# GEGLU block: the first 512 rows of x by transposing transfers, unit 0 for both halves ahead of unit 1's raw products

## Chip, cores and metric

One core of one Trainium2 chip. The time is that of one launch on the device in microseconds, the median of three runs. All five engines (TensorE = PE, VectorE = DVE, ScalarE = ACT, GpSimd = POOL, SyncE = SP) have an instruction queue of their own and wait for each other by semaphores.

## What is computed

```python
B, S, Dm, Df = 1, 2048, 1024, 3584      # all bf16
def reference(x, w_gate, w_up, w_down):
    g = jnp.einsum("bsd,df->bsf", x, w_gate)
    u = jnp.einsum("bsd,df->bsf", x, w_up)
    h = _gelu(g) * u                     # tanh form
    return jnp.einsum("bsf,fd->bsd", h, w_down)
```

## The kernel before

The 2048 rows of x are two passes p of two halves c of N = 512 rows. Dm is NKB = 8 blocks of 128 rows of the weights; PE needs x with these blocks on the partitions, so x is transposed: `XT[p, c][k]` is block k, 128 partitions by 512 rows. Df is 28 blocks of 128, taken in pairs: a *unit* u is 256 columns of w_gate and of w_up (`load_w(u)`).

Most of the work goes by Strassen-like products (seven for eight), whose operands are sums of blocks. For a unit, `s1` to `s4` are sums and differences of its weights' quarters, `sa` a cast of one; `t1` to `t4` are those of x's halves, `tb` a cast. They are made by DVE, POOL and ACT in fp32r, and PE multiplies them: `product(e, s2, t2)` and so on in `unit`. *Raw products* (`raw_products`) are products of bf16 weights and bf16 x as they came, needed by each unit before its sums; their first part is copied to `p1` by ACT (`snap`).

Unit 0 for pass 0 is made without sums (`plain`), since nothing can be made before x and weights are there: per half 32 products of 128x512, into banks 0 to 3 for half 0 and banks 4 to 7 for half 1. `finish` takes gelu of the gate banks (ACT), multiplies by the up banks (DVE) and stores to DRAM (SP).

The order is written out by hand: the queues of SP, DVE, POOL and PE keep the program's order, and ACT's too inside the blocks shown. All DMAs are issued by SP's queue, in program order, and each of eight semaphores in turn goes with a DMA: a DMA is issued only when the one eight before it has landed.

The start, as before.py has it:

- PE warms itself with 7 products of constants (`keep_warm`, line 871).
- SP issues four copies of 128 rows of x (line 797), then unit 0's weights in six pieces (line 817, row blocks 0-2, 2-5, 5-8 of gate and up), unit 1's weights (line 148), four *transposing* transfers for rows 512 to 1023 of x (line 811, 256 columns each, that is two row blocks of `XT[0, 1]`), unit 2's weights (line 146), and then those for rows 1024 on (`turn_some`).
- PE transposes the first 512 rows, 8 blocks for each of the four copies (`turn`, line 804), against an identity that POOL makes, into banks 4 to 7; DVE and ACT copy the result to `xT0` (line 807).
- PE: `plain` for half 0, first two row blocks in column halves of 256; unit 1's raw products; `plain` for half 1 (`rest_of_0`, called from the first item's `aside`); then unit 1's f32 products `s2 t2`, `s1 t1`, `s3 t3`, `s4 tb`.
- DVE makes unit 1's sums s1, s2, s4, then t1, t2, t3, t4. POOL makes s3, and then waits for t4 (`pool_behind`, line 198) before it begins the sums of unit 2.

The kernel's later part (the joint units of both passes, and the product with w_down) is not touched.

Of the kernel before, what the change touches and what calls it, by code (L numbers as in the profile page):

```python
# [7 lines left out]


@with_exitstack  # L10
def kernel(
# [31 lines left out]
    NS = N // P  # L43
    NPASS = S // (2 * N)
    NU = NFB // 2
    NWARM = 7
    JOINT = 3
    AHEAD = {(0, -2): 2, (0, -1): 2, (0, 1): 1, (1, -2): 1}
    DIVIDED7 = 5
# [21 lines left out]

    xT = [xpool.tile([P, NKB, N], bf16, name=f"xT{p}") for p in range(NPASS)]
    XT = {(p, 0): [xT[p][:, k] for k in range(NKB)] for p in range(NPASS)}
    XT2 = {(p, 0): lambda k, p=p: xT[p][:, k : k + 2] for p in range(NPASS)}
    h = [[None, None], [None, None]]

    wdn = w_down.rearrange("(kh j p) d -> p kh j d", kh=2, p=P)
# [10 lines left out]
    def late_half(p):  # L88
        if p:
            tile = hpool.tile([P, NJ, N], bf16, name="h01")  # L90
            XT[p, 1] = [tile[:, k] for k in range(NKB)]
            x_late.append(tile[:, :NKB])
            XT2[p, 1] = lambda k: tile[:, k : k + 2]
        else:
            tiles = [slot([P, 2, N], bf16, "x") for _ in range(KH)]
            XT[p, 1] = [tiles[k // 2][:, k % 2] for k in range(NKB)]
            XT2[p, 1] = lambda k: tiles[k // 2]

    def new_h(kh, c):
        h[kh][c] = hpool.tile([P, NJ, N], bf16, name=f"h{kh}{c}")  # L100
# [685 lines left out]


    warm = nc.const_aps.tensor(1.0, [P, N], bf16)
    ident = xpool.tile([P, P], bf16, name="ident")
    make_identity(nc, ident)  # L790

    def load_x(c):
        t = []
        for i in range(NS):
            xn = slot([P, Dm], bf16, "xn")
            r0 = c * N + i * P
            nc.sync.dma_start(out=xn, in_=x2[r0 : r0 + P, :])  # L797
            t.append(xn)
        return t

    def turn(xn, i):
        tp = bank[4 + i].bitcast(bf16).rearrange("p (k r) -> p k r", k=NKB)
        for ko in range(NKB):
            nc.tensor.transpose(tp[:, ko, :], xn[i][:, ko * P : (ko + 1) * P], ident)  # L804
        for ks in (range(NKB),) if i < NS - 1 else (range(KH), range(KH, NKB)):
            ks = slice(ks.start, ks.stop)
            (on_act if i == 1 else on_dve)(out=xT[0][:, ks, i * P : (i + 1) * P], in_=tp[:, ks])

    def transposing(p, c, k0):
        r0 = (2 * p + c) * N  # L810
        nc.sync.dma_start_transpose(
            out=XT2[p, c](k0), in_=x2[r0 : r0 + N, k0 * P : (k0 + 2) * P]
        )

    def load_wf(queue, k0, k1):
# [7 lines left out]
            if queue is not nc.sync:  # L823
                tc.keep_in_program_order(got)

    xn0 = load_x(0)
    wf = wpool.tile([P, 2, NKB, 2 * P], bf16, name="w")
    for k0, k1 in ((0, 2), (2, 5), (5, NKB)):
        load_wf(nc.sync, k0, k1)
    w = load_w(1)  # L830
    late_half(0)
    for ko in range(0, NKB, 2):
        transposing(0, 1, ko)
    ahead = load_w(2, True)
    late_half(1)
    turns = [(c, ko) for ko in range(0, KH, 2) for c in (1, 0)] + [(c, ko) for c in (1, 0) for ko in range(KH, NKB, 2)]
# [5 lines left out]

    turn_some(2)

    def plain(ps, c, kos, parts=1):
        n = N // parts
        for k in range(kos.start, kos.stop, 2):
            for part in range(parts):
                cols = slice(part * n, (part + 1) * n)
                for p, (j, i) in zip(ps, [(j, i) for j in range(2) for i in range(2)]):  # L850
                    for ko in (k, k + 1):
                        matmul(
                            p[:, cols],
                            wf[:, i, ko, j * P : (j + 1) * P],
                            XT[0, c][ko][:, cols],
                            ko == 0 and part == 0,
                            ko == NKB - 1,
                        )

# [1 line left out]
        for j in range(2):  # L861
            times(0, j, c, gelu(ps[2 * j]), ps[2 * j + 1])

    on_dve, on_act = nc.vector.tensor_copy, nc.scalar.copy
    s = sums_s(w, dve)
    t = sums_t(0, dve, lambda name: slot([P, N], f32r, name))
    T = [t, None]
    with tc.manual_schedule(engines={ENG.Activation}):
        def keep_warm(n, cols):
            for _ in range(n):  # L870
                nc.tensor.matmul(
                    bank[3][:, :cols], lhsT=warm[:, :P], rhs=warm[:, :cols], start=True, stop=True
                )

        keep_warm(NWARM, N)
        for i in range(NS):
            if i == 2:
                keep_warm(2, 2 * P)
            turn(xn0, i)
        plain(bank[0:4], 0, range(0, 2), parts=2)  # L880
        plain(bank[0:4], 0, range(2, NKB))
        s["s3"] = sums_s(w, pool)["how"]["s3"](s)
        s["s1"] = s["how"]["s1"](s, range(1))
        finish(bank[0:4], 0)
        s["s1"] += s["how"]["s1"](s, range(1, 2))
        nxt = {"p1": raw_products(odd, cc, 0, w)}
        s.make("sa", "s2", "s4")
        t.make("t1")

    seen = xpool.tile([P, 1], f32, name="seen")  # L890

    def rest_of_0(part):
        if part == 0:
            plain(bank[4:8], 1, range(NKB))
            t.make("t2", "tb")
        else:
            t3 = t["how"]["t3"](t, range(0, 2))
            finish(bank[4:8], 1)
            t["t3"] = t3 + t["how"]["t3"](t, range(2, KH))

    spots, twos = {}, {}

# [165 lines left out]
    with tc.manual_schedule(engines={ENG.Activation}):  # L1068
        for n, (u, p) in enumerate(items):
            first = n == 0  # L1070
            def after_p5():
                at_p5(n)

            def aside(part):
                if first and part < 0:
                    rest_of_0(part + 2)
                if first and part == 0:
                    t.make("t4")
                for v in loads.get((n, part), ()):
                    ws[v] = load_w(v, True)  # L1080
                turn_some(AHEAD.get((n, part), 0))
                if (n, part) == (1, -2):
                    two_sums("t2", XL[:, KH:], "t1")
                    two_sums("t3", XL[:, KH:], XL[:, :KH])

            def mid():
                if "sa" not in ss[u]:
                    ss[u]["sa"] = sums_s(loaded(u), pool)["how"]["sa"](None)

            def ahead_of_p4():  # L1090
                if n == 0:
                    raw_of(2, 0, even, cc)()
                elif n == 1:
                    p1 = [raw_first(e, 1, loaded(v)) for e, v in ((Eb, 2), (D, 1))]
                    raw_second(K, 1, loaded(2))
                    finish_raw(2, 1, K, p1[0])

                    T[1]["tb"] = spots["tb"]
                    for k in range(KH):
                        nc.scalar.copy(out=spots["tb"][k], in_=XT[1, 1][KH + k])  # L1100
                    new_room(0, 1, *["t4"] * KH, *["n"] * 3)
                    two_sums("t4", xT[1][:, KH:], "t2")
                    new_s(0, "s1", "s2", "s3", "s4")

                    def second_half():
                        raw_second(K, 1, loaded(1))
                        finish_raw(1, 1, K, p1[1])

                    nxt["c11"] = second_half
                elif n == 3:  # L1110
                    raw_of(0, 1, Ea, D)()

            def behind_p4():
                if "c11" in nxt:
                    nxt.pop("c11")()

            def p4(c12):
                times(p, 2 * u, 1, gelu(c12[0]), c12[1])
                if n == len(items) - 1:
                    split_b_rest("tb")  # L1120
                    more_room()
                    split_b("t4")
                whole_p4(u, p, banks[0], ss[u], ahead_of_p4, behind_p4)
                if n == len(items) - 1:
                    split_b_rest("t4")

            if first:
                banks = odd, cc, dd
                late = lambda: add(cc, nxt["p1"])
            else:  # L1130
                banks = (Eb, D, K) if n == 3 else (Ea, K, D)
                late = None
            unit(u, p, banks, ss[u], late, after_p5, aside, mid, p4)
            ss[u].pop("sa")
            if n == 1:
                Ea, Eb, K, D = Eb, D, K, Ea
            elif n == 3:
                Ea, Eb, K, D = Ea, K, D, Eb

# [68 lines left out]
```

## Time and profile before

| | |
|---|---|
| median of 3 runs | 526.49 us (526.41 to 526.50) |
| profiled execution, its own time | 526.39 us |
| its span, first to last instruction | 524.6 us |
| granted PE clock, mean | 1.00 |
| PE busy | 518.7 us (99%) |
| DVE, ACT, POOL busy | 390.6, 293.6, 336.9 us |
| HBM read, written | 72.61 MB, 29.62 MB |

In rows of the timeline the first number is the start in us from the span's start, the second the time from the start of the first to the end of the last of the merged instructions; then engine (SPq is SP's queue, issuing), line, operation, output<-inputs and shapes, how many, and in brackets how long the engine had been idle and what ended that. In rows of the chain: start, length, what. In windows: the stretch, its length, busy time and number of instructions of each engine, granted PE clock, share of the 16 DMA engines, GB/s. Matmuls' ends are modelled, and a few matmul records are missing.

### The profile page before, as it was taken

The page shows a single profiled execution, that of the slowest core. Times are in us where ns is not written, and L with a number is a line of the kernel's source. Part 1 is how long each engine was busy: PE and PEld are TensorE (multiplying, and loading weights), DVE is VectorE, ACT ScalarE, POOL GpSimd, SP SyncE. Part 2 cuts the span into 40 slices and gives each one's busy share as a digit, 9 for nine tenths or more (in the row PEclk, how much of TensorE's full clock was granted, in tenths as well). Part 3 has the DMA queues.
Part 4 walks back from the last instruction along what each step waited for, and adds up shares of the span by engine and source line. Part 5 has one row for each costly group of instructions (what it writes and reads, how often), then busy time and mean ns, then how long its engine had stood idle before and what let it go on. Part 6 is the DMA issues. An engine that isn't in the chain of part 4 may idle for free.

```text
span 524.6 us, 7866 instructions
## 1 busy us (share of the span) xinstructions
PE 518.7 (99%) x2356; PEld 368.0 (70%) x2389; DVE 390.6 (74%) x598; ACT 293.6 (56%) x542; POOL 336.9 (64%) x339
## 2 busy tenths in 40 slices
PE   9999999999999999999999999999999999999997
PEld 5576877767667676767677676754788885488887
DVE  2984553687888989897988889897789226967934
ACT  3556655676778687878787787851135602142430
POOL 1079999998999999999999999840000000000594
PEclk9999999999999999999999999999999999999999
DMA  9961323032625457373727444999976999993732
GB/s 252 213 166 52 89 84 111 32 109 92 191 81 181 123 180 230 112 239 111 233 92 231 163 159 159 343 374 415 385 259 212 394 398 353 392 327 101 238 133 71
DMA packets 102730, 105.91 MB, mean 202 GB/s; under 512 B 19360, under 2 KB 80800, under 8 KB 102688
## 3 DMA queue, kind: packets, MB, share of 16 engines
q1 hardware_dynamic: 102688, 105.41, 61.4%
q8 instruction: 19, 0.31, 0.3%
q14 instruction: 23, 0.19, 0.1%
HBM read 72.61 MB, written 29.62 MB: 195 GB/s over the span
## 4 chain that ended last, share of the span: by engine, by line
PE 98%; DMA 1%; issue 0%; SPq 0%; DVE 0%
PE bank L127 98%; DMA xn<-in_x_dram 1%; SPq L797 0%; PE bank L804 0%; DVE st L106 0%
## 5 line engine op out<-in xcount | busy, mean ns | idle before, releaser
L127 PE MATMUL bank<-h,s 128*128 128x512 f32 x500 | 132.6, 395 | 0.0
L109 POOL TENSOR_TENSOR q<-q 128x256 fp32r<-128x256 f32 x28 | 26.6, 984 | 144.4 <-DMA q<-td 143.8
L127 PEld LDWEIGHTS bank<-h,s 128*128 128x128 f32 x500 | 93.9, 188 | 21.1
L127 PE MATMUL bank<-xT,w 128*128 128x512 bf16 (+1 forms) x446 | 106.8, 376 | 1.5
L127 PEld LDWEIGHTS <-w 128*128 128x128 bf16 x504 | 45.4, 98 | 59.1 <-issue 11.9
L109 POOL TENSOR_TENSOR s<-w 128x512 fp32r<-128x512 bf16 (+1 forms) x76 | 77.8, 1040 | 10.4 <-DMA w<-in_w_gate_dram 10.3
L127 PE MATMUL bank<-t,s 128*128 128x512 f32 x276 | 76.5, 400 | 0.0
L127 PE MATMUL bank<-q 128*128 128x512 f32 x264 | 65.6, 390 | 0.0
L127 PEld LDWEIGHTS bank<-t,s 128*128 128x128 f32 x276 | 51.9, 188 | 12.1
L127 PEld LDWEIGHTS bank<-q 128*128 128x128 f32 x264 | 49.6, 188 | 10.4
L123 ACT COPY p<-bank 128x512 f32<-128x512 f32 x72 | 40.6, 589 | 28.9 <-PE bank L127 28.6
L106 DVE TENSOR_TENSOR q<-h,h 128x512 fp32r<-128x512 bf16 x56 | 38.3, 684 | 16.8 <-DMA h<-hd 16.8
L123 ACT COPY u<-bank 128x512 f32<-128x512 f32 x62 | 35.8, 589 | 21.1 <-PE bank L127 21.0
L109 POOL TENSOR_TENSOR s<-s,s 128x256 fp32r<-128x256 f32 x60 | 44.8, 769 | 1.6
L106 DVE TENSOR_TENSOR xz<-bank,xz 128x512 f32<-128x512 f32 x44 | 30.2, 691 | 18.2 <-PE bank L127 14.6
L127 PEld LDWEIGHTS <-h 128*128 128x128 bf16 x224 | 21.7, 98 | 26.5 <-issue 0.5
L109 POOL TENSOR_TENSOR s<-w,s 128x512 fp32r<-128x512 bf16 (+1 forms) x37 | 39.4, 1081 | 0.0
L109 POOL TENSOR_TENSOR s<-s,w 128x512 fp32r<-128x512 f32 (+1 forms) x37 | 37.3, 1024 | 0.9
L118 ACT CAST tb<-raw 128x512 fp32r<-128x512 bf16 x28 | 16.9, 632 | 36.0 <-DMA raw<-in_w_down_dram 26.5
L109 POOL TENSOR_TENSOR m<-raw,m 128x512 fp32r<-128x512 bf16 x28 | 34.5, 1234 | 2.2
L106 DVE TENSOR_TENSOR bank<-bank,u 128x512 f32<-128x512 f32 x49 | 33.7, 688 | 0.0
L106 DVE TENSOR_TENSOR v<-bank,v 128x512 f32<-128x512 f32 x44 | 29.2, 684 | 2.1 <-PE bank L127 1.7
(122 smaller groups left out, 911.7 us busy)
## 6 DMA issues: line engine op xcount, KB each, us to landing
raw<-in_w_down_dram SPq DMA_DIRECT2D x68, 256.0 KB, 4.0
q<-td SPq DMA_DIRECT2D x66, 256.0 KB, 5.4
td<-m SPq DMA_DIRECT2D x42, 256.0 KB, 2.8
hd<-o SPq DMA_DIRECT2D x80, 128.0 KB, 1.7
h<-hd SPq DMA_DIRECT2D x17, 512.0 KB, 6.9
hd<-h SPq DMA_DIRECT2D x30, 128.0 KB, 1.7
h<-hd SPq DMA_DIRECT2D x5, 768.0 KB, 9.0
out_dram<-st SPq DMA_DIRECT2D x30, 128.0 KB, 4.6
```

Source lines behind the costliest of these rows:

```text
L106: nc.vector.tensor_tensor(out=out, in0=a, in1=b, op=op)
L109: nc.gpsimd.tensor_tensor(out=out, in0=a, in1=b, op=op)
L118: nc.scalar.copy(out=t, in_=src)
L123: nc.scalar.copy(out=t, in_=ps)
L127: nc.tensor.matmul(ps, lhsT=lhs, rhs=rhs, start=start, stop=stop, skip_group_check=True)
```

## The change

The first 512 rows of x also come by transposing transfers of 256 columns, four, and they are first in SP's queue. Unit 0's weights come in eight pieces (two row blocks of gate, of up, four times) from ACT's queue, ahead of ACT's other work. In SP's queue unit 1's weights stand behind all eight transposing transfers. The copies of x, the identity, PE's transposes and their evictions are gone; PE warms with 8 products. `plain` takes the row blocks in pairs, the gate's two banks first and then the up's, always 512 columns wide, for half 0 and then at once for half 1; unit 1's raw products follow. DVE makes t1 first, then t2, half of t3, s1, s2, the rest of t3, and s4 and t4 behind unit 1's raw sum; ACT makes `tb` and `sa` ahead of the second half's gelu; POOL makes s3 when unit 1's weights are there.

```diff
-    NWARM = 7
+    NWARM = 8
+    FIRST = (0, 2), (2, 4), (4, 6), (6, NKB)
...
-    xn0 = load_x(0)
     wf = wpool.tile([P, 2, NKB, 2 * P], bf16, name="w")
-    for k0, k1 in ((0, 2), (2, 5), (5, NKB)):
-        load_wf(nc.sync, k0, k1)
-    w = load_w(1)
+    for k0, k1 in FIRST:
+        load_wf(nc.scalar, k0, k1)
+    for k0, k1 in FIRST:
+        transposing(0, 0, k0, k1 - k0)
     late_half(0)
     for ko in range(0, NKB, 2):
         transposing(0, 1, ko)
+    w = load_w(1)
     ahead = load_w(2, True)
...
-    def plain(ps, c, kos, parts=1):
-        n = N // parts
-        for k in range(kos.start, kos.stop, 2):
-            for part in range(parts):
-                cols = slice(part * n, (part + 1) * n)
-                for p, (j, i) in zip(ps, [(j, i) for j in range(2) for i in range(2)]):
+    def plain(ps, c):
+        for k in range(0, NKB, 2):
+            for i in range(2):
+                for j in range(2):
                     for ko in (k, k + 1):
                         matmul(
-                            p[:, cols],
+                            ps[2 * j + i],
                             wf[:, i, ko, j * P : (j + 1) * P],
-                            XT[0, c][ko][:, cols],
-                            ko == 0 and part == 0,
+                            XT[0, c][ko],
+                            ko == 0,
                             ko == NKB - 1,
                         )
...
         keep_warm(NWARM, N)
-        for i in range(NS):
-            if i == 2:
-                keep_warm(2, 2 * P)
-            turn(xn0, i)
-        plain(bank[0:4], 0, range(0, 2), parts=2)
-        plain(bank[0:4], 0, range(2, NKB))
+        plain(bank[0:4], 0)
+        plain(bank[4:8], 1)
+        t.make("t1")
+        finish(bank[0:4], 0)
+        t.make("t2", "tb")
+        t3 = t["how"]["t3"](t, range(0, 2))
         s["s3"] = sums_s(w, pool)["how"]["s3"](s)
-        s["s1"] = s["how"]["s1"](s, range(1))
-        finish(bank[0:4], 0)
-        s["s1"] += s["how"]["s1"](s, range(1, 2))
+        s.make("s1", "sa", "s2")
+        finish(bank[4:8], 1)
+        t["t3"] = t3 + t["how"]["t3"](t, range(2, KH))
         nxt = {"p1": raw_products(odd, cc, 0, w)}
-        s.make("sa", "s2", "s4")
-        t.make("t1")
...
-    def rest_of_0(part):
-        if part == 0:
-            plain(bank[4:8], 1, range(NKB))
-            t.make("t2", "tb")
-        else:
-            t3 = t["how"]["t3"](t, range(0, 2))
-            finish(bank[4:8], 1)
-            t["t3"] = t3 + t["how"]["t3"](t, range(2, KH))
...
             def aside(part):
-                if first and part < 0:
-                    rest_of_0(part + 2)
                 if first and part == 0:
+                    s.make("s4")
                     t.make("t4")
```

More of the change, by code (lines that the diff above doesn't have):

```diff
@@ L6 @@
 from concourse._compat import with_exitstack
-from concourse.masks import make_identity
 @with_exitstack
@@ L73 @@
     XT = {(p, 0): [xT[p][:, k] for k in range(NKB)] for p in range(NPASS)}
-    XT2 = {(p, 0): lambda k, p=p: xT[p][:, k : k + 2] for p in range(NPASS)}
+    XT2 = {(p, 0): lambda k, n, p=p: xT[p][:, k : k + n] for p in range(NPASS)}
     h = [[None, None], [None, None]]
@@ L92, in late_half @@
             x_late.append(tile[:, :NKB])
-            XT2[p, 1] = lambda k: tile[:, k : k + 2]
+            XT2[p, 1] = lambda k, n: tile[:, k : k + n]
         else:
@@ L96, in late_half @@
             XT[p, 1] = [tiles[k // 2][:, k % 2] for k in range(NKB)]
-            XT2[p, 1] = lambda k: tiles[k // 2]
+            XT2[p, 1] = lambda k, n: tiles[k // 2]
     def new_h(kh, c):
@@ L788, with transposing @@
     warm = nc.const_aps.tensor(1.0, [P, N], bf16)
[L789 to L793, printed above, removed]
-        for i in range(NS):
[L795 to L809, printed above, removed]
+    def transposing(p, c, k0, nk=2):
         r0 = (2 * p + c) * N
         nc.sync.dma_start_transpose(
-            out=XT2[p, c](k0), in_=x2[r0 : r0 + N, k0 * P : (k0 + 2) * P]
+            out=XT2[p, c](k0, nk), in_=x2[r0 : r0 + N, k0 * P : (k0 + nk) * P]
         )
@@ L862, in finish @@
             times(0, j, c, gelu(ps[2 * j]), ps[2 * j + 1])
-    on_dve, on_act = nc.vector.tensor_copy, nc.scalar.copy
     s = sums_s(w, dve)
@@ L875 @@
         keep_warm(NWARM, N)
-        for i in range(NS):
-            if i == 2:
-                keep_warm(2, 2 * P)
-            turn(xn0, i)
-        plain(bank[0:4], 0, range(0, 2), parts=2)
-        plain(bank[0:4], 0, range(2, NKB))
+        plain(bank[0:4], 0)
[4 more added lines that the diff above has]
+        t3 = t["how"]["t3"](t, range(0, 2))
         s["s3"] = sums_s(w, pool)["how"]["s3"](s)
-        s["s1"] = s["how"]["s1"](s, range(1))
-        finish(bank[0:4], 0)
-        s["s1"] += s["how"]["s1"](s, range(1, 2))
+        s.make("s1", "sa", "s2")
+        finish(bank[4:8], 1)
+        t["t3"] = t3 + t["how"]["t3"](t, range(2, KH))
         nxt = {"p1": raw_products(odd, cc, 0, w)}
-        s.make("sa", "s2", "s4")
-        t.make("t1")
     seen = xpool.tile([P, 1], f32, name="seen")
-    def rest_of_0(part):
-        if part == 0:
-            plain(bank[4:8], 1, range(NKB))
-            t.make("t2", "tb")
-        else:
-            t3 = t["how"]["t3"](t, range(0, 2))
-            finish(bank[4:8], 1)
-            t["t3"] = t3 + t["how"]["t3"](t, range(2, KH))
     spots, twos = {}, {}
```

## The prediction, made before the changed kernel ran

> **What bounds the kernel now.** I read the page's head and chain first, then the chain's start, then the timeline of the first 30 us.
>
> ```profile
> span 524.6 us, 7866 instructions
> PE 518.7 (99%) x2356; PEld 368.0 (70%) x2389; DVE 390.6 (74%) x598; ACT 293.6 (56%) x542; POOL 336.9 (64%) x339
> ...
> PE 98%; DMA 1%; issue 0%; SPq 0%; DVE 0%
> ```
> ```profile
> 2.12 4.03 DMA xn<-in_x_dram
> ...
> 6.20 0.62 PE bank L804 x8
> ...
> 7.08 1.70 PE bank L127 x14
> ...
> 8.84 10.74 PE bank L127 x49
> ```
> The chain is PE from 6.2 us to the end. Only its first 6.2 us are anything else: the four copies of x. So the change can move the end only by the moment from which PE runs without a gap, or by a gap that it opens; every edit lies in the first 30 us.
>
> ```profile
> 0.74 1.82 SPq L797 DMA_DIRECT2D xn<-in_x_dram  x4
> 0.77 3.15 PE L871 MATMUL bank<-const-bfloat16-1.0 128*128 128x512 bf16 x7 [0.77 <-PEq L1192]
> 3.71 1.30 PE L804 MATMUL bank<-ident,xn 128*128 128x128 bf16 x16
> 4.85 0.38 PE L871 MATMUL bank<-const-bfloat16-1.0 128*128 128x256 bf16 x2
> 5.50 1.32 PE L804 MATMUL bank<-ident,xn 128*128 128x128 bf16 x16 [0.27 <-DMA xn<-in_x_dram]
> 6.66 10.76 PE L127 MATMUL bank<-xT,w 128*128 128x256 bf16 x55
> 7.97 7.67 SPq L811 DMA_TRANSPOSE x<-in_x_dram  x4
> 17.25 7.07 PE L127 MATMUL bank<-x,w 128*128 128x512 bf16 x31
> 23.97 5.82 PE L127 MATMUL bank<-t,s 128*128 128x512 f32 x24
> ```
> Before 17.25 us PE has unit 0's first half (32 products of 512 columns, the first eight as sixteen of 256) and 16 raw products. From 8.84 to 19.58 there are 49 records and one gap in them, 50 steps: 0.216 us each. Counting 16 of these back from 17.25 gives 13.8 us as the end of unit 0's first half. From there 16 + 32 products lead to 24.2 us, where the first f32 product can begin (the row's 23.97 is within one product of it). This 13.8 is the mark: in both kernels 48 dense products follow before the f32 ones, only in another order. The end moves by what the mark moves, if nothing behind it becomes late.
>
> **The change, part by part.** Removed: four copies of x, the identity, 32 PE transposes (1.30 + 1.32 us) with two short warming products, and their evictions by DVE and ACT. They lie in PE's first 6.7 us, which end on x's arrival, so removing them gives nothing until something better arrives. Added: one warming product, (3.71 - 0.77)/7 = 0.42 us, so warming ends at 4.1 us; hidden if the first x comes later.
>
> x's first half now comes by four transposing transfers, first in SP's queue; unit 0's weights by eight 128 KB transfers, first in ACT's queue. Products of pair k of row blocks wait for transfer k and both of its weight pieces. Eight products of a pair take 8 x 0.216 = 1.73 us.
>
> ```profile
> L811 SPq DMA_TRANSPOSE xT<-in_x_dram x1: 1237/1237/1237, 38.1 to 38.1; - x1
> ...
> DMA to landing us min/median/max: 3.1/3.1/3.1
> ```
> This one, alone, landed 3.1 us after issue. The first x could land at 0.74 + 3.1 = 3.9 us; beside weights, twice its 1.24 us share, 5.1. PE would start some 1.5 us earlier than 6.66. But then it needs a pair each 1.73 us. What a pair costs is read from windows of transfers:
>
> ```profile
> core 0: us, PE busy (x) PEld busy (x) DVE busy (x) ACT busy (x) POOL busy (x), PEclk, DMA share, GB/s
> 0.00:2.00 2.00, 1.23 (x3) 0.44 (x4) 0.00 (x0) 1.27 (x1) 0.70 (x6) 1.00 0.04 7
> 10.00:12.00 2.00, 2.00 (x11) 0.90 (x10) 0.49 (x1) 0.00 (x0) 0.44 (x1) 1.00 1.21 290
> 12.00:13.00 1.00, 1.00 (x7) 0.45 (x5) 0.20 (x1) 0.29 (x1) 1.00 (x1) 1.00 1.35 211
> 13.00:14.00 1.00, 1.00 (x6) 0.43 (x5) 0.66 (x1) 0.73 (x2) 0.84 (x2) 1.00 1.25 280
> 16.00:18.00 2.00, 2.00 (x11) 0.94 (x10) 2.00 (x5) 1.35 (x3) 0.00 (x0) 1.00 1.17 50
> 18.00:19.00 1.00, 1.00 (x7) 0.41 (x6) 1.00 (x2) 0.55 (x2) 0.00 (x0) 1.00 0.84 198
> 22.00:23.00 1.00, 1.00 (x6) 0.49 (x5) 1.00 (x3) 0.00 (x0) 0.00 (x0) 1.00 1.47 219
> 26.00:27.00 1.00, 1.00 (x6) 0.84 (x5) 1.00 (x3) 0.80 (x2) 0.00 (x0) 1.00 1.07 234
> 40.80:41.20 0.40, 0.40 (x3) 0.33 (x2) 0.00 (x0) 0.40 (x2) 0.40 (x1) 1.00 0.00 0
> ```
> The last columns are the share and GB/s. Weight copies alone move 290; transposing transfers alone 234 to 280; where the two meet (12:13, 18:19, 22:23) 211, 198, 219, mean 209; and 16:18, in the middle of transposing ones, fell to 50. No row shows both kinds from two queues at once. Bounds: 280 to 290 if they don't disturb each other, 100 or less if they stall each other; I take 209, the nearest rows. The first half needs 1.05 MB of x and 1.05 MB of weights: 2.10/0.209 = 10.0 us from 2.0 us (the first window moved 7 GB/s) = 12.0. Last packet to landing I take as 0.6: the transfer issued at 38.1 landed at 41.2, and 40.8:41.2 moved nothing. So the last pair lands at 12.6, its products end at 14.4: **+0.6 us** on the mark.
>
> Beside this row stands the Trainium skill, "DMA: Bandwidth & Descriptors", section "Latency and other measured facts": a transposing transfer's effective rate is 261 GB/s. By it, and 290 for copies, the last pair would land at about 10.2 and the mark would be 2 us earlier; the windows 22:23 and 12:13 don't agree, since there copies stand beside it.
>
> Pairs then come each 0.52 MB/0.209 = 2.5 us against 1.73 of work: PE waits 0.8 us between them. In the trace PE's products take 0.42 us each until 4 us and 0.216 afterwards, while the column PEclk reads 1.00 in both: a half rate which that column does not show. PE gets to 4.1 us warm, idles until about 5.1, and then works some two thirds of the time. If one pair falls back to the half rate it takes 3.4 us, 1.0 more than the transfers need; that cost is nothing if it never happens, 1.7 in the last pair, 3 for two pairs. I take **+1.0 us**.
>
> Behind the mark, with its cover:
> - x's second half: four more transposing transfers from 12.6 on, 0.262/0.234 = 1.1 us each against 1.73 of products. Hidden; without it each late one costs its lateness.
> - Unit 1's weights now come behind all eight: 12.0 + 4 x 1.1 + 1.05/0.29 = 20.0, landed at 20.6. Raw products need the first at 14.4 + 6.9 = 21.3. Slack 0.7 us.
> - ACT's order puts the casts of these weights ahead of the gelus of the second half and the copies p of the raw products, for which the first f32 product waits.
>
> ```profile
> 13.57 0.60 ACT L221 ACTIVATE g<-bank 128x512 f32<-128x512 f32 x1 [0.27 <-PE bank L127]
> ...
> 15.41 1.29 DVE L106 TENSOR_TENSOR s<-s,w 128x512 fp32r<-128x512 f32 x2
> ...
> 16.21 1.14 ACT L118 CAST sa<-w 128x512 fp32r<-128x512 bf16 x2
> ...
> 27.43 2.49 DVE L106 TENSOR_TENSOR t<-xT,t 128x512 fp32r<-128x512 bf16 x4
> ...
> 29.98 0.18 POOL L198 COPY seen<-t 128x1 f32<-128x1 f32 x1 [15.46 <-DVE t L106]
> ...
> 31.67 3.40 PE L127 MATMUL bank<-xT,w 128*128 128x512 bf16 x15
> ...
> 39.11 4.30 POOL L109 TENSOR_TENSOR h<-h,xT 128x1024 fp32r<-128x1024 bf16 x2
> ```
> Casts 20.6 to 21.7, then four of 0.6 us: 24.1, needed at 14.4 + 6.9 + 3.5 = 24.8. Covered by 0.7 us.
> - DVE: s1, s2 move behind t2, s4 behind the raw sum. Of s1 and s2 four of 1.29/2 us follow the landing at 20.6: 23.2, before 24.8. t4 releases POOL, before at 29.98, 5.8 us after 24.2. Now two raw sums, two of s4 and four of t4 (2.49) follow the raw products' end: 4 x 0.65 + 2.5 = 5.1 us behind the f32 start. No cost.
> - Transfer waits of the new order: the last weight piece is issued only when the second x has landed (about 7.5), 3 us before use; the fourth x waits for the first. Hidden.
> - SP: the transposing transfers for rows 1024 on are queued behind stores that wait for both finished halves, about 24 us; POOL reads them at 39.1 us. Hidden by 10 us. Unit 2's weights follow unit 1's by 3.6 us, 24.2; PE reads them at 31.7. Hidden.
>
> Sum: +0.6 +1.0 = +1.6 on a profiled execution of 526.39 us (span 524.6 and 1.8 around it); the median of the runs, 526.49, is 0.1 above. Rounded: **527.9**, own range 527.0 to 528.8.
>
> **Rivals.** A difference within 0.2% (1.05 us) is about what a measurement of this kernel can't tell from none.
> 1. *Two queues fill the engines, no loss.* For: 280 and 290 GB/s alone; against: the meeting rows. From 245 to 285 GB/s the last pair lands at 11.2 to 10.0, the mark falls at 12.9 to 11.9 (no earlier, as 5.1 + 6.9 = 12.0): -0.9 to -1.9, **525.1**. It decides when the last pair lands before 12.1 us. Faster.
> 2. *PE keeps its full rate through the waits.* Only +0.6 (or -0.9 to +0.6 with a better rate): **526.9**. The rule of the Trainium skill, "TensorE: Matmul & The Clock Gate", section "Part 1: The HAM clock gate", says this: the rate falls after an idle window of about 3.4 us, and gaps of 0.8 are shorter. For it in the trace: PE idled from 5.1 to 5.5 and the products behind ran at 0.216.
> 3. *Weights of unit 1 late.* A stall as in 16:18 (2 us at 50 instead of 209: 1.5 us lost) in either stream uses up the 0.7 us of slack, and the casts hold up gelus and copies on ACT: +1.6 + 1.5 = **529.5**.
> 4. *It doesn't do what it says*: the queue's slot waits make ACT's weights follow x in turn. Then the streams are not beside each other, and the sum is rival 1's lower rate, about 526.
>
> **How the numbers follow.** Forecast 0.40 (slower), rival 3 0.15 (slower), rival 1 0.25 (faster), rivals 2 and 4 0.20 (within). So faster 0.25, within 0.20, slower 0.55. The range takes in most of rivals 1 and 3: 525.0 to 529.9.
>
> **What would show it.** In the profile after: first bf16 product on xT near 5 us; then pairs of eight with waits on the transposing transfers; windows of 5 to 12 us near 209 GB/s with both kinds of transfer; the last of the first 32 products near 14 to 15 us; products 0.42 us apart somewhere after 5 us; the first f32 product near 25.8 against 24.2; no other gap to the end. Wrong if the first 32 products end before 13 us, if 0.42 never recurs, or if PE shows a wait on s, t or w behind the raw products.

## The result, and the profile after

The changed kernel takes 527.41 us (median of 18 runs, 526.94 to 528.15), the kernel before, run beside it, 526.55 (18 runs, 526.21 to 527.48): a ratio of 1.0018, 95% interval 1.001 to 1.0025. It is 0.5 to 1.3 us slower: the way that was forecast, by about half of the 1.6 us. The profiled execution took 527.61 us against 526.39.

The head and the chain's shares on the page of the changed kernel, and the waits of PE that the trace lists (total, times, longest, in us):

```profile
span 525.8 us, 7806 instructions
PE 520.0 (99%) x2348; PEld 365.6 (70%) x2348; DVE 388.8 (74%) x594; ACT 290.7 (55%) x540; POOL 338.0 (64%) x337
...
PE 93%; DVE 0%; issue 0%
```
```profile
PE bank L127 <- DMA xT<-in_x_dram: 1.7, 2, 1.4
...
PE bank L127 <- DVE h L106: 0.4, 1, 0.4
```

PE's share of the chain fell from 98 to 93%, though its busy time rose. The chain is followed back only to the last place where PE waited, and that is now at 34 us instead of 6:

```profile
34.35 0.01 DVE sum L106
...
34.40 5.77 PE bank L127 x25
```

So there is a second wait, behind everything that the prediction priced. The timeline has both (start, length from first to last of the merged instructions, in brackets the idle time before):

```profile
0.78 3.57 PE L849 MATMUL bank<-const-bfloat16-1.0 128*128 128x512 bf16 x8 [0.78 <-PEq L1158]
...
5.79 5.01 PE L127 MATMUL bank<-xT,w 128*128 128x512 bf16 x16 [1.44 <-DMA xT<-in_x_dram]
...
11.02 3.61 PE L127 MATMUL bank<-xT,w 128*128 128x512 bf16 x16 [0.22 <-DMA xT<-in_x_dram]
...
14.47 7.07 PE L127 MATMUL bank<-x,w 128*128 128x512 bf16 x32
...
19.54 4.06 POOL L109 TENSOR_TENSOR s<-w 128x512 fp32r<-128x512 bf16 x2 [19.10 <-DMA w<-in_w_gate_dram]
...
20.34 0.68 DVE L106 TENSOR_TENSOR s<-w 128x512 fp32r<-128x512 bf16 x1
...
21.30 1.28 DVE L106 TENSOR_TENSOR s<-w 128x512 fp32r<-128x512 bf16 x1 [0.28 <-DMA w<-in_w_up_dram]
...
22.51 2.24 DVE L106 TENSOR_TENSOR s<-s,w 128x512 fp32r<-128x512 f32 x2
...
24.64 5.83 PE L127 MATMUL bank<-t,s 128*128 128x512 f32 x24
...
32.13 1.90 PE L127 MATMUL bank<-xT,w 128*128 128x512 bf16 x8
...
33.08 1.27 DVE L106 TENSOR_TENSOR h<-g,bank 128x512 bf16<-128x512 f32 x2
...
34.40 1.89 PE L127 MATMUL bank<-xT,w 128*128 128x512 bf16 x8 [0.37 <-DVE h L106]
```

Three things are to be seen. The mark, the end of unit 0's first half, is where the products on `x` begin: 14.47 in place of 13.80, +0.67. The first pair of row blocks ran slowly: its seven first products take 3.06 us, while the ten from 8.30 on take 2.50,

```profile
5.79 3.06 PE L127 MATMUL bank<-xT,w 128*128 128x512 bf16 x7 [1.44 <-DMA xT<-in_x_dram]
```
```profile
8.30 2.50 PE L127 MATMUL bank<-xT,w 128*128 128x512 bf16 x10
```

but PE then still waits 0.22 us at 11.02 for the third transfer (landed at 10.97), so the slowness ended inside another wait. And at 34.40 PE waits for a bank that DVE's `h` has still to read. The 0.37 us in the bracket count from the modelled end of the product before; from start to start the wait costs more: 34.40 - 32.13 - 8 x 0.216 = 0.54 us. 0.67 + 0.54 = 1.21 is the whole 1.2 us between the two spans.

Transfers from 2 to 12 us (last columns: share of the 16 DMA engines, GB/s):

```profile
2.00:4.00 2.00, 2.00 (x6) 0.76 (x5) 0.00 (x0) 0.00 (x0) 0.00 (x0) 1.00 1.09 260
4.00:6.00 2.00, 0.56 (x2) 0.10 (x1) 0.00 (x0) 0.00 (x0) 0.00 (x0) 1.00 1.14 165
6.00:8.00 2.00, 2.00 (x6) 0.73 (x5) 0.00 (x0) 0.00 (x0) 0.00 (x0) 1.00 1.28 199
8.00:10.00 2.00, 2.00 (x10) 0.78 (x9) 0.00 (x0) 1.26 (x1) 0.00 (x0) 1.00 1.26 224
10.00:12.00 2.00, 1.78 (x9) 0.77 (x8) 0.00 (x0) 0.03 (x1) 0.00 (x0) 1.00 1.26 279
```

Their mean is 225 GB/s, at a share above 1 throughout. The four transfers of the first half landed at 5.75, 8.30, 10.97 and 11.64.

### The profile page after: what moved, and what is told of

It is laid out like the page before. It is cut to its first block, busy times and chain, and to the rows that moved or that the text cites. A ratio compares the mean times of both kernels' runs of the same rounds, so it can differ in the third digit from the quotient of the medians.

```text
span 525.8 us, 7806 instructions
## 1 busy us (share of the span) xinstructions
PE 520.0 (99%) x2348; PEld 365.6 (70%) x2348; DVE 388.8 (74%) x594; ACT 290.7 (55%) x540; POOL 338.0 (64%) x337
## 3 DMA queue, kind: packets, MB, share of 16 engines
q10 hardware_dynamic: 2176, 1.05, 1.0%
## 4 chain that ended last, share of the span: by engine, by line
PE 93%; DVE 0%; issue 0%
PE bank L127 93%; DVE st L106 0%; DVE sum L106 0%
## 5 line engine op out<-in xcount | busy, mean ns | idle before, releaser
L127 PE MATMUL bank<-xT,w 128*128 128x512 bf16 x464 | 110.4, 384 | 2.0 <-DMA xT<-in_x_dram 1.7
L109 POOL TENSOR_TENSOR s<-w 128x512 fp32r<-128x512 bf16 (+1 forms) x76 | 78.9, 1053 | 19.2 <-DMA w<-in_w_gate_dram 19.1
L109 POOL TENSOR_TENSOR s<-s,s 128x256 fp32r<-128x256 f32 x60 | 47.2, 808 | 1.6
L109 POOL TENSOR_TENSOR m<-raw,m 128x512 fp32r<-128x512 bf16 x28 | 33.8, 1207 | 2.2
L106 DVE TENSOR_TENSOR bank<-bank,u 128x512 f32<-128x512 f32 x49 | 33.7, 689 | 0.7 <-PE bank L127 0.7
```

Source lines behind the costliest of these rows:

```text
L106: nc.vector.tensor_tensor(out=out, in0=a, in1=b, op=op)
L109: nc.gpsimd.tensor_tensor(out=out, in0=a, in1=b, op=op)
L127: nc.tensor.matmul(ps, lhsT=lhs, rhs=rhs, start=start, stop=stop, skip_group_check=True)
```

## The experiments

Theory: the new start costs, since its 2.1 MB pass no faster than some 209 GB/s and reach PE in pieces that come too late; and DVE, made late, costs again at 34 us. Rivals: the half rate of PE costs; the new order costs; two queues cost where one would not.

**The start alone**, with the order before (unit 1's weights ahead of x's second half, `rest_of_0` behind unit 1's raw products):

```diff
-        transposing(0, 0, k0, k1 - k0)
+        transposing(0, 0, k0)
+    w = load_w(1)
...
-    w = load_w(1)
```

> The new start (x's first half by transposing transfers, weights from ACT's queue, 8 warming products) with the old order behind it: unit 1's weights ahead of x's second half in SP's queue, raw products between unit 0's halves, sums as before. Theory: the changed kernel's loss has two parts, the mark (end of unit 0's first half, 14.47 against 13.80 us) and a wait of PE at 34 us for VectorE, whose chain is late because unit 1's weights land at 21.3. Here only the first is left: mark 14.4 to 14.6, no wait for VectorE, +0.7 us on before. Rival (the order is a gain, the start costs all of the loss and more): at least +1.2 us on before, slower than the changed kernel.

Measured: 527.75 us (11 runs, 526.58 to 528.24), before 526.75, ratio 1.0016 [1.0008, 1.0025].

```profile
7.62 6.50 PE L127 MATMUL bank<-xT,w 128*128 128x512 bf16 x28 [0.45 <-DMA xT<-in_x_dram]
...
14.82 2.76 PE L127 MATMUL bank<-xT,w 128*128 128x512 bf16 x11 [0.71 <-DMA w<-in_w_up_dram]
```

The profiled execution (526.58) was the fastest of its eleven. Its transfers moved 244 GB/s from 2 to 10 us, its third transfer of x landed at 9.41, and 16 products later, at about 12.9, is its mark: earlier than in the kernel before. Nothing is lost at 34 us, but PE waits 0.71 us for unit 1's weights. So this profile does not show what the slower ten lost; by the medians the start costs as much alone (+1.0) as with the new order (+0.9).

**The order alone**, with the copies and PE transposes of before:

> The kernel before with the other part of the change alone: x's second half ahead of unit 1's weights in SP's queue, unit 0 for both halves first, then unit 1's raw products, and the sums in the changed kernel's order. Theory (the order costs only by unit 1's late weights, whose sums on VectorE meet POOL's s3): weights land at about 17, not 21.3, VectorE is in time, no wait at 34 us: within 0.2 us of before. Rival (the order itself costs the 0.4 to 0.5 us behind the mark): 0.4 us or more slower than before, with a wait of PE for VectorE near 33 us.

Measured: 526.99 us (11 runs), before 526.77, ratio 1.0002 [0.9994, 1.0011].

```profile
14.50 7.07 PE L127 MATMUL bank<-x,w 128*128 128x512 bf16 x32
...
18.02 2.25 DVE L106 TENSOR_TENSOR t<-x 128x512 fp32r<-128x512 bf16 x2
...
20.19 2.24 DVE L106 TENSOR_TENSOR s<-w 128x512 fp32r<-128x512 bf16 x2
...
24.68 5.84 PE L127 MATMUL bank<-t,s 128*128 128x512 f32 x24
```

No cost can be measured, and PE shows no wait behind the mark, although two pairs of DVE's sums are slow here too (2.25 and 2.24 for 1.28 elsewhere): unit 1's last weights landed at 20.12, 1.2 us earlier than in the changed kernel, with the same start of the f32 products (24.68 and 24.64). With the run before it, this puts the loss on the start, and the wait at 34 us on the start making these weights late.

This profile shows one thing more. Its mark is 14.50, although its start is that of the kernel before, with the mark at 13.80: the fourth copy of x landed at 6.88 in place of 6.15. So launches of the old start alone differ by as much as the 0.67 between the two profiles, and what the start costs is known from the medians, not from one profile of each.

**13 warming products** in place of 8, so that PE works until the first transfer lands:

```diff
-    NWARM = 8
+    NWARM = 13
```

> The changed kernel with 13 warming products in place of 8, so that PE is busy until the first x lands at 5.8. Theory: the first pair's half rate (eight products 0.427 us apart) is hidden, since the third x lands only at 10.97 and its two pairs set the mark: first pair at 0.216, mark still 14.4 to 14.5, time as the changed kernel's within 0.2 us. Rival (the half rate costs what the prediction took for it, 1.0 us, in this run or in those of the changed kernel's runs that took 528): 0.4 to 1.0 us faster, and the runs closer together.

Measured: 528.25 us (6 runs), ratio 1.0027 [1.0016, 1.0038]; no product on `xT` at the half rate, and the mark at 14.76: the third transfer landed at 11.27, and 16 products of 0.216 later is 14.7. Curing the half rate gains nothing that can be seen here; a wait of 1.97 us, at 9.32, takes its place. Unit 1's last weights landed at 21.78, and the wait at 34 to 35 us is 0.81 in the bracket.

**x nearly alone**: three quarters of unit 0's weights come behind unit 1's, and the products read the first quarter in their place. So a part of the sum is left out; the number of products stays.

```diff
-    for k0, k1 in FIRST:
+    for k0, k1 in FIRST[:1]:
         load_wf(nc.scalar, k0, k1)
...
     w = load_w(1)
+    for k0, k1 in FIRST[1:]:
+        load_wf(nc.sync, k0, k1)
...
-                            wf[:, i, ko, j * P : (j + 1) * P],
+                            wf[:, i, ko % 2, j * P : (j + 1) * P],
```

> The changed kernel with only the first two row blocks of unit 0's weights ahead; the other six blocks come behind unit 1's weights, and unit 0's products of pass 0 use the first two blocks for all (this part of the computation is left out). So the transposing transfers have the engines to themselves. Theory (the engines are shared, and that paces x): x lands 1.3 to 1.4 us apart, the last at 8 to 8.5 us, PE runs from 4.5 us on without a wait, mark 11.3 to 11.8, 2 to 2.6 us faster than before. Rival (a transposing transfer is slow by itself, or its issue is): x lands 2 us or more apart as in the changed kernel, mark 14 or later, no gain.

Measured: 525.88 us (12 runs), ratio 0.9985 [0.9973, 0.9997], six runs from 524.71 to 525.28 and six from 526.48 to 527.40. The profiled one is of the upper six:

```profile
0.77 3.57 PE L851 MATMUL bank<-const-bfloat16-1.0 128*128 128x512 bf16 x8 [0.77 <-PEq L1160]
6.22 8.74 PE L127 MATMUL bank<-xT,w 128*128 128x512 bf16 x32 [1.88 <-DMA xT<-in_x_dram]
```

The four transfers were there at 6.18, 6.92, 7.96 and 9.29, and still the 32 products take 8.74 us where 7.07 is the full rate. With the data there, the half rate costs 1.7 us.

**The same with 14 warming products:**

> As x_alone (three quarters of unit 0's weights come after x's second half, and the first 64 products read the first two row blocks of the weights in place of their own, so that part of the sum is left out), with 14 warming products, until about 6.7 us. Theory that the half rate makes x_alone's two groups of runs: PE comes warm to the first pair, no product after 6.7 us is 0.42 us apart, the upper group (526.5 to 527.4) goes, the runs lie between 524.6 and 525.8 and their median about 0.9 us below x_alone's 525.88; the mark falls at 13.2 us or earlier. Rival, the landing of the transposing transfers alone makes the groups: the two groups and the median of 525.9 stay, though no product is 0.42 us apart.

Measured: 524.98 us (5 runs, 524.83 to 525.45), before 526.83, ratio 0.9968 [0.9956, 0.9981].

```profile
5.28 7.07 PE L127 MATMUL bank<-xT,w 128*128 128x512 bf16 x32
```
```profile
6.00:8.00 2.00, 2.00 (x11) 0.90 (x10) 0.00 (x0) 0.00 (x0) 0.00 (x0) 1.00 0.98 205
8.00:10.00 2.00, 2.00 (x11) 0.88 (x9) 0.00 (x0) 0.00 (x0) 0.00 (x0) 1.00 1.09 196
```

The upper group is gone, the median is 0.9 lower, as the theory of the half rate asked, and PE has no gap at all. Since the first transfer also landed earlier here (5.24 against 6.18), the two profiles alone don't prove it; the groups do so only as far as five runs can. The second fence shows something else: transposing transfers alone move 196 to 205 GB/s.

**One queue**: unit 0's weights in SP's queue too, two pieces ahead of each transfer of x, and 10 warming products.

```diff
-    NWARM = 8
+    NWARM = 10
...
-    for k0, k1 in FIRST:
-        load_wf(nc.scalar, k0, k1)
     for k0, k1 in FIRST:
+        load_wf(nc.sync, k0, k1)
         transposing(0, 0, k0, k1 - k0)
```

> The changed kernel with unit 0's weights in SP's queue too, each pair of pieces directly ahead of its transposing transfer, and 10 warming products. So copies and transposing transfers follow each other on one queue and are never side by side. Theory (what paces x is that two queues of different kinds stand side by side on the same engines; alone each kind moves 235 to 290 GB/s): x lands about 2.2 us apart by issue (0.47 + 0.47 + 1.24), the first at 5 to 5.5, the last at 11.6 to 12, with little spread between runs; mark 13.3 to 13.8, 0.6 to 1.1 us faster than the changed kernel, about as before or faster. Rival (changing between the kinds costs the same in one queue): last x at 12.5 or later, mark 14.4 or later, no faster than the changed kernel.

Measured: 528.92 us (5 runs, 528.75 to 529.24), before 526.77, ratio 1.004 [1.0028, 1.0052]. x landed at 5.23, 7.93, 10.18 and 12.79, and the mark is 14.55, where the change has 14.47 and, in a second profile below, 14.98. The theory that two queues side by side cost falls: one queue is no earlier at the mark. Its further loss lies behind the mark: unit 1's last weights landed at 22.48, the f32 products begin at 25.44 in place of 24.64, and the wait at 34 to 35 us is 0.85. Its runs are closer together than the change's.

**Weights first**, then x, all in SP's queue, 14 warming products:

> The changed kernel with all of unit 0's weights first in SP's queue, then x's transposing transfers, and 14 warming products. One change of kind only. Theory (sharing is what costs): weights done by 6 us, x lands at about 7.4, 8.7, 9.9, 11.1, PE starts at 7.4 and never waits: mark 14.2 to 14.4, the fourth x 0.5 to 1 us earlier than the changed kernel's 11.64, though four copies' worth of time is spent ahead of the first. Time as the changed kernel's or 0.3 us less, with less spread. Rival (transposing transfers are slow by themselves): x 2 us or more apart, last at 13 or later, mark 15 or later, 0.5 us or more slower than the changed kernel.

Measured: 529.97 us (6 runs), ratio 1.0057 [1.0045, 1.007].

```profile
10.00:12.00 2.00, 2.00 (x11) 0.93 (x10) 0.00 (x0) 0.00 (x0) 0.00 (x0) 1.00 1.17 188
12.00:14.00 2.00, 2.00 (x11) 0.94 (x10) 0.00 (x0) 0.00 (x0) 0.00 (x0) 1.00 1.33 194
```

x landed each 1.5 to 1.7 us with nothing beside it, 188 to 194 GB/s, between the theory's 1.2 and the rival's 2; the mark is 15.41. So transposing transfers are slow without copies beside them. Whether the DMA engines or the issuing sets this rate is open. In the run with x nearly alone and 14 warming products, SP's queue needed 1.30 us to issue each of the next four (min/median/max in ns):

```profile
L791 SPq DMA_TRANSPOSE x<-in_x_dram x4: 1300/1301/1302, 6.4 to 10.4; - x4
```

0.262 MB each 1.30 us are 202 GB/s, about what was measured, so one queue could hardly have given more. No run changed the time of an issue.

**Only the weights' queue**: the kernel before with `load_wf(nc.scalar, k0, k1)`.

> The kernel before with one part of the change alone: unit 0's weights from ACT's queue (its six pieces), x still by copies and PE's transposes. Theory (two queues share the engines): weights take half of the engines from the copies of x, the last copy lands at about 7.5 to 8.5 in place of 6.15, PE's first product moves from 6.66 to 8 to 9, the rest is dense: 1.2 to 2 us slower than before. Rival (a second queue adds bandwidth or only saves issue time): the last copy lands within 0.3 us of 6.15, time as before or faster.

Measured: 531.17 us (6 runs), ratio 1.0085 [1.0067, 1.0102], far more than forecast.

```profile
9.58 0.72 PE L804 MATMUL bank<-ident,xn 128*128 128x128 bf16 x8 [2.55 <-DMA xn<-in_x_dram]
```
```profile
10.00:11.00 1.00, 1.00 (x9) 0.73 (x7) 0.66 (x2) 0.00 (x0) 0.00 (x0) 0.50 1.22 295
```

The fourth copy of x, issued only at 3.93 us, landed at 9.53 instead of 6.15; all six pieces of weights landed before it, the last at 8.74. That moves the first product on `xT` from 6.66 to 10.09, 3.4 us. The products on `x` begin at 22.08 in place of 17.25, 4.8 us later. The other 1.4 us are the half rate, and here the column PEclk, third from the end, shows it: 0.50 from 10 to 13 us, 0.81 from 13 to 14. Before the wait of 2.55 us the column read 1.00, and the eight transposes behind it still ran at the full rate (their weights were loaded in 0.46 us, in the kernel before in 0.45). Five of the six runs list a mean clock of 0.994 to 0.997; the one at 1.000 took 529.23, the least.

**POOL's s3 held behind DVE's s2**, so that it no longer runs beside DVE's sums of weights:

```diff
+    seen = xpool.tile([P, 1], f32, name="seen")
...
-        s["s3"] = sums_s(w, pool)["how"]["s3"](s)
         s.make("s1", "sa", "s2")
+        nc.gpsimd.tensor_copy(out=seen, in_=s["s2"][-1][:, 0, :1].bitcast(f32))
+        s["s3"] = sums_s(w, pool)["how"]["s3"](s)
```

> The changed kernel with POOL's two s3 sums held until VectorE has made s2. Theory: VectorE's sums s1, s2 of unit 1 (1.28 and 1.64 us in place of 0.68) are slowed by POOL's s3, which runs beside them and reads the same weights; alone they take 0.68, VectorE is about 1.5 us earlier, PE's wait of 0.37 us at 34 us goes, 0.4 us faster than the changed kernel. Rival (the transfers into SBUF slow them, or the late weights alone make the wait): the sums stay at 1.2 to 1.6 us and the time stays.

Measured: 527.52 us (11 runs), ratio 1.0011 [1.0002, 1.002].

```profile
24.09 2.73 POOL L109 TENSOR_TENSOR s<-w 128x512 fp32r<-128x512 bf16 x2
...
24.91 2.45 DVE L106 TENSOR_TENSOR t<-x 128x512 fp32r<-128x512 bf16 x2
...
34.61 1.89 PE L127 MATMUL bank<-xT,w 128*128 128x512 bf16 x8 [0.44 <-DVE h L106]
```

s1 and s2 are at 0.69 again, but now t3's second half is slow (2.45 for two, 1.28 elsewhere). The slow sums move with s3, and the wait stays.

**s3 held behind t3**, one step further:

> The change, with POOL's s3 held until DVE has made the second half of t3. Theory that s3 beside DVE's sums makes DVE late and so PE wait at 34 us: no sum of DVE from two operands in SBUF takes more than 0.7 us between 20 and 26 us, DVE is some 1.5 us earlier at t4, PE's wait of 0.37 to 0.44 us at 34 us is gone, and the time is 0.3 to 0.4 us below the change's. Rival, the wait hangs on the late weights alone, or s3 is now late itself: the wait at 34 us stays or one on s stands at about 28.4 us, and the time is the change's or more.

Measured: 527.31 us (11 runs), before 526.83, ratio 1.0012 [1.0003, 1.0021].

```profile
26.00 2.74 POOL L109 TENSOR_TENSOR s<-w 128x512 fp32r<-128x512 bf16 x2
...
26.83 2.45 DVE L106 TENSOR_TENSOR s<-w,s 128x512 fp32r<-128x512 bf16 x2
...
34.13 1.89 PE L127 MATMUL bank<-xT,w 128*128 128x512 bf16 x8 [0.42 <-DVE h L106]
```

As expected no sum is slow before 26 us, but s4, straight behind, is. DVE was not made earlier, the wait stayed, and the gain of 0.3 to 0.4 us was not shown: the median lies 0.1 below the change's 527.41 and 1.0 below the 528.27 of its second set of runs, and those two sets differ by as much. Three places of s3 thus slow three different sums. A place beside DVE's work on banks was not tried.

**The change once more**, a second set of runs:

> The change once more, unaltered, on the chip of the three others. Theory that the landing of the first transposing transfers differs from launch to launch and sets the mark: the runs spread from 526.9 to 528.2 as before, and in a second profile the first four landings differ by up to 1 us from 5.75, 8.30, 10.97 and 11.64, with the mark moved by what the third or fourth moved. Rival, the start is the same each time and the spread comes from elsewhere: the landings agree within 0.2 us and the mark is 14.5 again.

Measured: 528.27 us (9 runs, 527.32 to 528.85), before 526.83, ratio 1.0024 [1.0014, 1.0034].

```profile
0.77 3.22 PE L849 MATMUL bank<-const-bfloat16-1.0 128*128 128x512 bf16 x8 [0.77 <-PEq L1158]
...
5.40 1.89 PE L127 MATMUL bank<-xT,w 128*128 128x512 bf16 x8 [1.41 <-DMA xT<-in_x_dram]
...
9.15 1.89 PE L127 MATMUL bank<-xT,w 128*128 128x512 bf16 x8 [1.86 <-DMA xT<-in_x_dram]
...
11.53 3.61 PE L127 MATMUL bank<-xT,w 128*128 128x512 bf16 x16 [0.50 <-DMA xT<-in_x_dram]
...
35.61 1.89 PE L127 MATMUL bank<-xT,w 128*128 128x512 bf16 x8 [0.86 <-DVE h L106]
```

The transfers landed at 5.36, 9.11, 11.49 and 12.53. The third moved by +0.52 and the mark by +0.51, to 14.98; unit 1's last weights came at 22.37 in place of 21.28 and the wait at 34 to 35 us grew to 0.86 in the bracket. No product was at the half rate, and this execution (528.85) is slower than the first one (527.61), which had it. The landings differ from launch to launch as the theory said; the medians of the two sets differ by more than expected, while their ratios' intervals overlap.

**Copies in column halves** (a try at a better start): the kernel before, with x copied as 512 columns of all rows, four pieces of weights, the other 512 columns, the other weights; PE transposes in two halves.

> The kernel before, with its first 512 rows copied in two halves of 512 columns: first halves of all four row groups, unit 0's weights of row blocks 0 to 3, second halves, the other weights; PE transposes in two halves. Theory that the start is bound by bytes, and that plain copies carry them without the loss of transposing transfers: PE begins its products some 1.5 us earlier, works while the second half lands, and the mark falls at about 13.3 in place of 13.8: 526.0 to 526.2. Rival: ten issues of SP in place of the first eight, or the 32 transposes and their evictions, which no longer hide behind x's arrival (16 x 0.08 = 1.3 us more on the path): the same or up to 1 us slower than the kernel before.

Measured: 527.54 us (11 runs), ratio 1.0012 [1.0003, 1.0021]: slower.

```profile
12.34 3.84 PE L127 MATMUL bank<-xT,w 128*128 128x512 bf16 x17 [1.10 <-DMA w<-in_w_up_dram]
```

PE began its products at 5.87, 0.8 earlier than in the kernel before, and then waited 1.10 for weights that landed at 12.30; the products on `x` begin at 18.83, so the mark, 16 products earlier, is 15.4 and not the theory's 13.3. The transfers moved 240 to 265 GB/s between 2 and 8 us, where those of the kernel before moved 316 and 325 between 2 and 6. That the copies' rows, half as long, are the reason was not tested apart. No version tried that does all the work beats the kernel before.

## Why the prediction was right or wrong, point by point

- **The bytes at 209 GB/s, +0.6 on the mark.** Right in size: from 2 to 12 us 225 GB/s moved on the mean and the mark moved by 0.67; in the second profile of the change it was 196 GB/s and 1.18. The place was off: the prediction let the last pair set it (12.6 + 1.73), the trace shows the third. In both profiles the third transfer's landing plus 16 x 0.216 gives the mark: 10.97 + 3.46 = 14.43 (14.47), 11.49 + 3.46 = 14.95 (14.98); so it does with 13 warming products (14.73, 14.76) and with s3 behind t3 (14.09, 14.16). The prediction's even spacing of 2.5 us put that landing at 10.1, 0.9 too early, and the last one at 12.6, 1.0 too late. That +0.6 meets +0.67 so closely is partly luck.
- **The rate of transposing transfers.** The rows chosen for them alone (234 to 280) were too kind: alone at the start they move 188 to 205, and the row with 280 (13 to 14 us) has a copy beside them, since unit 1's last weights landed at 13.30 there. That is also below the 261 GB/s that the Trainium skill, "DMA: Bandwidth & Descriptors", section "Latency and other measured facts", gives for pieces that are not contiguous; the measurement decides. Rival 1 needed 245 to 285 GB/s for both kinds together. The two profiles of the change stayed below that, with 225 and 196; the fastest launch of the start alone came to it, with 244 and a mark of about 12.9, which is where rival 1 has it. So rival 1 is not how this start usually goes, but it is not out of reach of a single launch. What x alone would be worth, 1.9 us by the medians, is seen only where three quarters of the weights stay away.
- **+1.0 us for one pair at the half rate.** This is the term that failed. The half rate came, at the pair after the warming, but cost nothing there: the third transfer was awaited anyway, as the gap of 0.22 at 11.02 shows. In the run with s3 held behind s2, where it lasted ten products, the mark was 14.62 against 10.95 + 3.46 = 14.41 from the third landing: 0.2 us. The prediction charged it on top of waits that hide it. Its mechanism was wrong as well: the rate did not fall back in the gap, it had not yet risen. Eight warming products take 3.57 us in the three profiles where the half rate follows (the change, x alone, s3 behind s2) and 3.22 to 3.41 in the three where it does not (the change once more, the start alone, s3 behind t3), because in the latter the last one already ran faster; after that, gaps of up to 2.02 us left the full rate untouched. The column PEclk agrees: it reads 1.00 over the slow pair, as over the warming, and 0.50 only in the run with the weights' queue alone, where the rate did fall, behind a wait of 2.55 us. So what the prediction feared exists, but this start's gaps are too short for it. Its own sign, products 0.42 us apart after 5 us, is there in the first profile of the change and missing in the second. So rival 2's sum, +0.6 and nothing for the rate, is what the start measured.
- The Trainium skill, "TensorE: Matmul & The Clock Gate", "Part 1: The HAM clock gate", has both halves of this: the rate rises after a busy window of about 3.4 us that runs free of the kernel, and falls after an idle one. On the second the runs agree in part: no gap of up to 2.0 us brought the half rate back once the full one was reached, but one of 2.55 us, shorter than that window, with eight short transposes on either side, did; the measurement decides. On the first, 3.22 us of warming was in one launch enough and 3.57 in another not.
- **"No cost" for DVE.** Wrong by 0.5 to 1.0 us from start to start, in the two profiles of the change. The trace of before held a warning, in rows that the prediction did not use:

```profile
11.51 0.69 DVE L106 TENSOR_TENSOR s<-w 128x512 fp32r<-128x512 bf16 x1 [3.90 <-DMA w<-in_w_gate_dram]
11.56 1.65 POOL L109 TENSOR_TENSOR s<-w 128x512 fp32r<-128x512 bf16 x1 [10.25 <-DMA w<-in_w_gate_dram]
13.34 0.69 DVE L106 TENSOR_TENSOR h<-g,bank 128x512 bf16<-128x512 f32 x1 [1.14 <-ACT g L221]
13.37 1.15 POOL L109 TENSOR_TENSOR s<-w 128x512 fp32r<-128x512 bf16 x1 [0.15 <-DMA w<-in_w_up_dram]
...
31.04 1.27 DVE L106 TENSOR_TENSOR h<-g,bank 128x512 bf16<-128x512 f32 x2
...
31.44 3.14 PEld L127 LDWEIGHTS <-w 128*128 128x128 bf16 x16 [0.26 <-issue]
```

  POOL's sum takes 1.65 beside a DVE sum of two SBUF operands and 1.15 beside one that reads a bank. Its first rows already show that the two hold each other up. In the change s3 meets s1 and s2: DVE's sum at 21.30 takes 1.28 and the pair at 22.51 takes 2.24, for 0.69 and 1.28: 1.55 us lost. The rest of DVE's lateness is the prediction's own count: behind the f32 start it named 5.1 us of work and left out the second half's `h` and t3's rest, 1.27 + 1.28. So `h` begins at 33.08 in place of 31.04, 2.04 later, against a mark 0.67 later. Before, the bank was free at 31.04 + 1.27 = 32.31 and needed by the ninth of the sixteen products whose weights are loaded from 31.44 on, at 31.45 + 1.73 = 33.18: a slack of 0.87. 2.04 - 0.67 - 0.87 = 0.50; the wait is 0.54.

  The slowed sums alone do not make this wait. The run with the order alone lost 1.9 us of DVE to them and had none. What it had is earlier weights: from the landing of unit 1's last weights to the end of these two `h` it is 13.1 us there (20.12 to 33.24) and 13.1 us in the change (21.28 to 34.35), and in all seven profiles with this wait the product that waits starts 12.8 to 13.4 us after that landing. By the forecast landing, 20.6, `h` would end at 33.7, just ahead of its need at 33.8 (the forecast mark, 14.4, and the 19.4 us from the change's mark to this product without its wait). The weights came 0.7 later, because their 1.05 MB took 4.7 us behind the last transfer of x (16.61 to 21.28, 225 GB/s) where the prediction took 290 GB/s. By this working both are needed, the slowed sums and the late weights; no run has the late weights without a slowed sum, so that part is worked out and not shown.
- The Trainium skill, "SBUF — State Buffer", "SBUF: two separate sides", gives the rule: a DVE operation with two SBUF inputs and a GpSimd operation share ports, and the one that comes second is blocked for the whole of the other. The runs agree: the sums lost 0.59 and 0.96 us, each less than one POOL sum of 1.15, and the sum that read a bank beside POOL kept its 0.69.
- **Unit 1's weights, slack 0.7; ACT; SP; POOL.** The weights landed at 21.28 (forecast 20.6) and PE did not wait for them at its raw products: right, with less to spare (these began at 21.37). ACT and SP show no wait of PE. Rival 3, a stall that makes PE stop for these weights, did not happen; the lateness went through DVE instead.
- **The sum.** +0.67 and +0.54 measured in one profile, +0.6 and +1.0 predicted (526.39 + 1.6 is 528.0, not the 527.9 written). The direction and the first term were right; the second term was a cost that lay hidden, and a smaller one took its place that had been put at nothing. That the total still comes out on the right side and not far off is in part luck, since the larger of its two terms cost nothing.

## What to carry to other kernels

A cost that lies ahead of a wait is charged only where it outlasts that wait: place the half rate, or any slowness, on the line of landings before adding it. For pieces that arrive one after another, take the latest of "landing plus the work that remains" over all pieces, not the last piece alone. Before moving a VectorE sum, look what GpSimd runs beside it and whether both read SBUF, and count every operation that the engine has until its next deadline. And before two profiles are compared, know how far launches of one kernel differ: here by as much as the effect.

## What was not expected of the hardware

- The moment at which PE's rate doubles differs by launch: near 3.5 us (the change once more), and only during the last of 14 warming products, about 6.4 us, in the run with weights first.
- Transposing transfers alone moved 188 to 205 GB/s at a share of 0.98 to 1.33 in the rows shown, while whole rows copied in the kernel before moved 316 and 325. Issuing one of 256 columns by 512 rows takes SP's queue 1.30 us.
- PEclk reads 1.00 while PE has not yet reached its full rate, and 0.50 when it has fallen back from it (the run with the weights' queue alone, from 10 us).
- The first four landings differ by up to 0.9 us between two launches of the same kernel. Why was not found out.
